# A decode step with attention and a gated MLP: chunks of T, S and PV interleaved, and w_out spread unevenly over the partitions

## Chip, core and metric

The kernel runs on one core of a Trainium2 chip. The metric is the device time of one execution in microseconds (us). Three runs of the kernel before gave 130.85, 130.9 and 132.37 us; their median, 130.9 us, is the time before.

## What is computed

One token `x` (1 x 576) is normalised, and the result goes through two branches whose outputs are added to `x`:

```
xn = layernorm(x)
A:  q = xn @ wq                       # 32 heads of 128, 16 key/value heads
    k, v = the last 4096 rows of k_cache, v_cache     # per key/value head, 4096 x 128
    o = softmax(q k^T / sqrt(128)) v ; A = o @ wo     # wo is 4096 x 576
B:  z = gelu(xn @ w_in)               # 576 x 4608
    z1, z2 = halves of z (2304 each)
    h = z1 * (w_sp * layernorm(z2) + b_sp) ; B = h @ w_out    # w_out is 2304 x 576
out = x + A + B
```

All inputs are bfloat16. With one token every matrix is used once, so the work is to read 51 MB from HBM: 16.8 MB of keys, 16.8 MB of values, 4.7 MB of wq, 5.3 MB of w_in, 4.7 MB of wo and 2.65 MB of w_out.

## The kernel before

**Loads.** SyncE (queue SP) issues every large load in the order of the list `order` (L103), and after it four loads of w_out (L117). Two key/value heads make one unit of 2 MB: `k0` to `k7` and `v0` to `v7`, each a tile of 128 partitions with 16 KB on each. `win1` to `win3` are thirds of w_in and `wo0` to `wo3` quarters of wo. All of these tiles come from the pool `units` (L60), which has 8 buffers: the ninth load can only be issued when the PE has finished with the first tile, and so on round the ring. A load reuses the semaphore of the load eight places ahead of it, so that SP also waits for that one to have landed. Behind SP's issues the loads stand in one hardware queue, spread over 16 DMA engines. Two single elements (`w_sp`, `b_sp`, L380) and the row `x` are loaded from ScalarE's queue.

**Attention by pairs of units.** Pair j is the units 2j and 2j+1. A unit has 8 chunks n of 8 blocks of 128 x 128. `T(n)` (L225) transposes the 8 blocks of a key chunk on the PE into PSUM and copies them to SBUF as kT (VectorE, or ScalarE for chunks 1, 4, 6 of eight). `S(n)` (L237) multiplies kT with the query into the scores of the pair. `sm_max`, `sm_tr`, `sm_exp` and `sm_rec` are the softmax: maximum per partition, a transpose to get it over the partitions, exponential, sum and reciprocal. `PV(b)` (L283) multiplies the 64 blocks of a value unit with the probabilities; `O_perm(j)` brings the result into the order of wo's rows, and `WO(j)` (L306) multiplies it with a quarter of wo, 32 small matmuls that accumulate in `out_ps`.

**MLP.** `z_part(b)` (L314) is a third of xn @ w_in, `gelu` runs on VectorE and ScalarE, `z_gate` (L346) makes the gated vector g and moves it from "element p + 128 c on partition p" to "18 consecutive elements on each partition" with 18 small matmuls: `row_of` (built by GpSimd, L146 to L151) holds 18 selection matrices, `col_of` (L215) the position inside a partition, and the result is `hv`. The last loop (L432) multiplies each of hv's 18 columns with the matching rows of w_out: 18 times 4 matmuls into `out_ps`. Row r of w_out's 18 on a partition sits in `wout_t[r]`, loaded in four parts of 8, 6, 3 and 1 rows.

**Order of the PE.** The order is written by hand (L396). In the part of pair j the PE first runs T of all 16 chunks of pair j+1, then S of all 16, then the stage's list: PV, z parts, permutations and WO of pair j, with the steps of the next softmax between them. After the last stage come the matmuls of w_out, one copy of `out_ps` to SBUF (L436) and the store of the output (L437).

**GpSimd** builds the identity (L121) at the very start and then `row_of`. VectorE waits for the identity before it builds the small masks (L129 to L160), and those stand in its program ahead of the normalisation of x, whose result `xe` the first projection needs (L196, L370).

Of the kernel before, what the change touches and what calls it, by code (L numbers as in the profile page):

```python
# [8 lines left out]
FP32 = mybir.dt.float32  # L9
# [21 lines left out]
OW = D // NCG  # L31
NWO = 4
FR = FH // P
UNITS = 8
KTB = 20
NEG = -1e30


# [1 line left out]
def kernel(  # L40
# [34 lines left out]
    wq_v = A_wq.rearrange("k (s c) -> (k s) c", s=2).rearrange("(p r) c -> p r c", r=NS)  # L75
    win_v = B_w_in.rearrange("k (s c) -> (k s) c", s=2).rearrange("(p r) c -> p r c", r=NS)
    wo_v = A_wo.rearrange("(j p r) n -> j p (r n)", p=P, r=8)
    wout_v = B_w_out.rearrange("(p r) n -> p r n", r=FR)


    def load_kv(store, cache, name, b, parts=1):
# [8 lines left out]
    def load_rows(store, view, name, width, cuts):  # L90
        for a, e in zip(cuts, cuts[1:]):
            t = units.tile([P, e - a, width], BF16, name=f"{name}{a}", tag="u")
            nc.sync.dma_start(t[:], view[:, a:e, :])
            for i in range(a, e):
                store[i] = t[:, i - a, :]

    def load_wo(j):
# [2 lines left out]
        wo_t[j] = t  # L100

    win_parts = {1: (0, 3), 2: (3, 6), 3: (6, 9)}
    order = ["wq1", "k0", "k1", "wq2", "k2", "k3", "v0", "win1", "v1", "win2", "k4", "k5", "v2", "win3", "v3", "wo0",  # L103
             "k6", "k7", "v4", "wo1", "v5", "wo2", "v6", "v7", "wo3"]
    for what in order:
        name, n = what.rstrip("0123456789"), what[-1]
        if name == "k":
# [6 lines left out]
            load_rows(win_t, win_v, "win", FH, win_parts[int(n)])  # L114
        else:
            load_wo(int(n))
    load_rows(wout_t, wout_v, "wout", D, (0, 8, 14, 17, 18))  # L117


    ident = const.tile([P, P], BF16, name="ident")  # L120
# [22 lines left out]
    selr = const.tile([P, 8, 8, 16], BF16, name="selr")  # L143


    row_of = const.tile([P, FR, P], BF16, name="row_of")  # L146
    nc.gpsimd.memset(row_of[:], 1.0)
    nc.gpsimd.affine_select(out=row_of[:], in_=row_of[:], compare_op=ALU.is_ge, fill=0.0, base=0,
                            pattern=[[P, FR], [-FR, P]], channel_multiplier=1)
    nc.gpsimd.affine_select(out=row_of[:], in_=row_of[:], compare_op=ALU.is_ge, fill=0.0, base=FR - 1,  # L150
                            pattern=[[-P, FR], [FR, P]], channel_multiplier=-1)  # L151
    rem = const.tile([P, 2, FR], FP32, name="rem")
    col_of = const.tile([P, FR, FR], BF16, name="col_of")
    out_ps = ps_c.tile([P, OW], FP32, name="out_ps")
    nc.vector.memset(out_ps[:], 0.0)

# [49 lines left out]
        return xe_r[:, 2 * r:2 * r + 2]  # L206

    nc.vector.tensor_copy(selr[:], ident[:].rearrange("p (q r) -> p r q", r=8).unsqueeze(2).to_broadcast([P, 8, 8, 16]))
    whole = P // FR * FR
    nc.vector.tensor_reduce(out=rem[:, 0, :], in_=ident_f[:, 0:whole].rearrange("p (q k) -> p k q", k=FR), axis=AXX, op=ALU.add)  # L210
    nc.vector.tensor_add(rem[:, 0, 0:P - whole], rem[:, 0, 0:P - whole], ident_f[:, whole:P])
    nc.vector.tensor_copy(rem[:, 1, :], rem[:, 0, :])
    rem_r = rem[:].rearrange("p a k -> p (a k)")
    for c in range(FR // 2):
        nc.vector.tensor_copy(col_of[:].rearrange("p (b c) r -> p c b r", b=2)[:, c],  # L215
                              rem_r[:, FR - 2 * c:2 * FR - 2 * c].unsqueeze(1).to_broadcast([P, 2, FR]))


    kT, s_ps, p_sb, sm = {}, {}, {}, {}
# [56 lines left out]
    def sm_rec(j):  # L276
        su = ps_m.tile([P, 8], FP32, name=f"su{j}", tag="m")
        nc.tensor.matmul(su[:], lhsT=ones_f[:], rhs=sm[j]["ss"][:].rearrange("p i c -> p (i c)"), start=True, stop=True)  # L278
        rm = work.tile([P, 8], FP32, name=f"rm{j}", tag="rm")
        nc.vector.reciprocal(rm[:], su[:])  # L280
        sm[j]["rm"] = rm

    def PV(b):  # L283
        j, i = divmod(b, 2)
        o = ps_o.tile([P, 4], FP32, name=f"o{b}", tag="o")
        for t in range(NT):
            nc.tensor.matmul(o[:], lhsT=vn[b][:, t, :], rhs=p_sb[j][:, i, t, :], start=t == 0, stop=t == NT - 1)  # L287
        with nc.allow_low_precision(reason="the attention's output is bfloat16 in the reference"):
            nc.vector.tensor_tensor(out=oTn[:, 4 * b:4 * b + 4], in0=o[:], in1=sm[j]["rm"][:, 4 * i:4 * i + 4], op=ALU.mult)  # L289

    def O_perm(j):
        op = ps_m.tile([P, 8, 8], FP32, name=f"op{j}", tag="m")
# [15 lines left out]
            out_mm(oP[:, j, r:r + 1], wo_t[j][:, D * r:D * (r + 1)])  # L308


    hv = const.tile([P, FR], BF16, name="hv")
    zacc = const.tile([P, FR, 2], FP32, name="zacc")

    def z_part(b):  # L314
# [31 lines left out]
    def z_gate(G, sz):  # L346
        sp = ps_m.tile([P, 2], FP32, name="sz_ps", tag="m")
        nc.tensor.matmul(sp[:], lhsT=ones_f[:], rhs=sz[:], start=True, stop=True)
        mz = rstd_of(sp[:], FH, "mz")
        gz = work.tile([P, FR], FP32, name="gz")  # L350
        nc.vector.tensor_scalar(out=gz[:], in0=G[:, 1, :], scalar1=mz[:, 0:1], scalar2=mz[:, 3:4],
                                op0=ALU.subtract, op1=ALU.mult)
        nc.vector.tensor_scalar(out=gz[:], in0=gz[:], scalar1=wb[:, 0:1], scalar2=wb[:, 1:2],
                                op0=ALU.mult, op1=ALU.add)
        g = work.tile([P, FR], BF16, name="g")
        nc.vector.tensor_mul(g[:], G[:, 0, :], gz[:])
        spread = const.tile([P, FR, FR], BF16, name="spread")
        nc.vector.tensor_tensor(out=spread[:], in0=col_of[:], in1=g[:].unsqueeze(2).to_broadcast([P, FR, FR]), op=ALU.mult)
        hp = ps_m.tile([P, FR], FP32, name="hp", tag="m")
        for c in range(FR):  # L360
            nc.tensor.matmul(hp[:], lhsT=row_of[:, c, :], rhs=spread[:, c, :], start=c == 0, stop=c == FR - 1)
        nc.vector.tensor_copy(hv[:], hp[:])


# [20 lines left out]
    for n in range(2 * NCH):  # L385
# [6 lines left out]

    stages = [["v0", "z1", "v1", "perm0", "z2"], ["v2", "z3", "v3", "perm1", "wo0"],  # L396
              ["v4", "wo1", "v5", "perm2", "wo2"], ["v6", "v7", "perm3", "wo3"]]
    for j, stage in enumerate(stages):
        if j == 0:
            sm_tr(0)  # L400
        if j + 1 < len(stages):
            for n in range(2 * NCH * (j + 1), 2 * NCH * (j + 2)):
                T(n)
                if n % 16 == 2 and j == 0:
                    sm_exp(0)
                if n % 16 == 8 and j == 0:
                    sm_rec(0)
            for n in range(2 * NCH * (j + 1), 2 * NCH * (j + 2)):
                S(n)
            sm_max(j + 1)  # L410
        for k, what in enumerate(stage):
            name, n = what[:-1], int(what[-1])
            if name == "v":
                PV(n)
            elif name == "z":
                z_part(n)
            elif name == "perm":
                O_perm(n)
            else:
                WO(n)  # L420
            if j + 1 < len(stages):
                if k == 0:
                    sm_tr(j + 1)
                elif k == 1:
                    sm_exp(j + 1)
                elif k == 2:
                    sm_rec(j + 1)
            if what == "z3":
                G, sz = gelu()
            if what == "v3":  # L430
                z_gate(G, sz)
    for j in range(FR):  # L432
        out_mm(hv[:, j:j + 1], wout_t[j], last=j == FR - 1)

    res = const.tile([P, OW], BF16, name="res")
    nc.vector.tensor_copy(res[0:97, :], out_ps[0:97, :])  # L436
# [31 lines left out]
```

## Time and profile before

| what | value |
|---|---|
| median of three runs | 130.9 us |
| the profiled execution, its own time | 131.38 us |
| its span, first to last instruction | 129.6 us |
| PE matmul busy | 92.8 us (72%) |
| VectorE busy | 57.8 us (45%) |
| ScalarE busy | 28.7 us (22%) |
| GpSimd busy | 7.1 us, all before 7.92 us |
| read from HBM | 50.96 MB, 393 GB/s over the span |
| mean granted TensorE clock | 0.73 |

The page of the profile gives the busy time of each engine and a picture of the span in 40 slices of 3.24 us, in tenths; the line DMA is the mean busy share of the 16 DMA engines. The chain of waits follows the work that ended last back to the start; "issue" in it is time in which the engine waited for nothing that the profile shows. A table of stretches gives for each engine the busy time and, in the last two columns, the busy share of the DMA engines and their rate in GB/s. Times in these views count from the first instruction.

### The profile page before, as it was taken

To read this page: it belongs to the slowest core of one execution; us is meant where nothing else is said; L and a number is where in the kernel's file an instruction comes from. 1 tells how busy PE (TensorE), PEld (TensorE's weight loads), DVE (VectorE), ACT (ScalarE), POOL (GpSimd) and SP (SyncE) were. 2 spreads that over 40 slices of the span, in tenths; PEclk is the share of its full clock that TensorE was granted. 3 is DMA by queue.
4 is the path that set the end of the run, shared out by engine and by line. 5 is a ranking of instruction groups with operands and counts; after the bars stand their busy time and mean duration, and the time that the engine had idled before them with its cause. 6 is when DMAs were issued, how large, how long until landed. Compare 5 with 4: busy or idle time off the path is not lost.

```text
span 129.6 us, 4571 instructions
## 1 busy us (share of the span) xinstructions
PE 92.8 (72%) x2135; PEld 86.2 (67%) x2135; DVE 57.8 (45%) x146; ACT 28.7 (22%) x34; POOL 7.1 (5%) x9
## 2 busy tenths in 40 slices
PE   3013999984798896585999993921989994878290
PEld 3013998874797786574988792921979792768190
DVE  6976758500658722252267421375367422420100
ACT  3001146500056710010155500101075400100000
POOL 7940000000000000000000000000000000000000
PEclk9999999995559996555579985555599955555555
DMA  4999999999999999999999999999999999999820
GB/s 132 430 392 438 455 415 400 445 427 420 430 416 427 431 411 425 444 410 435 420 409 438 428 411 429 430 425 425 408 431 426 416 444 415 420 402 419 333 106 0
DMA packets 4495, 51.23 MB, mean 395 GB/s; under 512 B 509, under 2 KB 638, under 8 KB 1022
## 3 DMA queue, kind: packets, MB, share of 16 engines
q1 hardware_dynamic: 4472, 50.96, 93.7%
q8 instruction: 16, 0.26, 0.8%
q14 instruction: 1, 0.01, 0.0%
q10 hardware_dynamic: 6, 0.00, 0.0%
HBM read 50.96 MB, written 0.00 MB: 393 GB/s over the span
## 4 chain that ended last, share of the span: by engine, by line
PE 57%; DVE 16%; issue 12%; ACT 11%; POOL 0%; ACTq 0%; POOLq 0%
PE tp L230 20%; PE s L245 10%; ACT kT L232 9%; PE o L287 9%; PE out_ps L303 5%; PE zp L319 3%; PE q_ps L370 3%; DVE other L141 2%; DVE d L268 2%; DVE ss L273 2%; DVE ident_f L129 2%; ACT p L270 1%; DVE own L137 1%; PE bc L264 1%; DVE kT L234 1%
## 5 line engine op out<-in xcount | busy, mean ns | idle before, releaser
L230 PE MATMUL tp<-ident,k 128*128 128x128 bf16 x512 | 39.5, 245 | 2.7 <-ACT kT L232 1.9
L230 PEld LDWEIGHTS <-k 128*128 128x128 bf16 x512 | 36.9, 113 | 5.0 <-issue 4.3
L234 DVE COPY kT<-tp 128x1024 bf16<-128x1024 bf16 x40 | 26.7, 689 | 15.1 <-PE tp L230 14.9
L232 ACT COPY kT<-tp 128x1024 bf16<-128x1024 bf16 x24 | 23.7, 1014 | 37.8 <-PE tp L230 37.7
L287 PE MATMUL o<-p,v 128*128 128x4 bf16 x512 | 15.4, 166 | 9.1 <-issue 8.8
L287 PEld LDWEIGHTS <-v 128*128 128x128 bf16 x512 | 14.5, 104 | 9.8 <-issue 9.7
L245 PEld LDWEIGHTS <-kT 128*128 128x128 bf16 x512 | 13.3, 97 | 3.1 <-issue 3.1
L245 PE MATMUL s<-q_bf,kT 128*128 128x4 bf16 x512 | 13.8, 165 | 2.1 <-issue 2.1
L270 ACT ACTIVATE p<-d 128x512 bf16<-128x512 f32 x4 | 2.5, 630 | 32.8 <-DVE d L268 32.8
L250 DVE TENSOR_REDUCE mx<-s 128x8 f32<-128x512 f32 x4 | 2.8, 692 | 14.7 <-PE s L245 14.7
L289 DVE TENSOR_TENSOR oTn<-o,rm 128x4 bf16<-128x4 f32 x8 | 1.3, 160 | 16.9 <-PE o L287 16.9
L303 PE MATMUL out_ps<-wo,oP 128*1 128x144 bf16 x128 | 4.8, 318 | 3.0 <-issue 1.8
L303 PEld LDWEIGHTS <-oP 128*1 128x1 bf16 x128 | 3.3, 113 | 3.6 <-issue 2.3
L370 PEld LDWEIGHTS <-wq 128*128 128x128 bf16 x144 | 4.1, 101 | 2.3 <-issue 2.3
L370 PE MATMUL q_ps<-xe,wq 128*128 128x2 bf16 x144 | 4.0, 164 | 2.2 <-DVE xe L196 2.2
L319 PEld LDWEIGHTS <-win 128*128 128x128 bf16 x162 | 4.9, 105 | 0.3 <-issue 0.2
L319 PE MATMUL zp<-xe,win 128*128 128x2 bf16 x162 | 4.8, 166 | 0.1
L273 DVE TENSOR_REDUCE ss<-p 128x8 f32<-128x512 bf16 x4 | 2.7, 686 | 2.8 <-ACT p L270 2.8
L168 PE MATMUL x_ps<-x,twice 64*128 64x9 bf16 x1 | 0.2, 166 | 5.3 <-DVE x L166 5.3
L168 PEld LDWEIGHTS <-twice 64*128 64x128 bf16 x1 | 0.1, 101 | 5.4 <-DVE x L166 5.4
L278 PE MATMUL su<-ss,ones_f 128*128 128x8 f32 x8 | 2.1, 332 | 1.3 <-DVE u L329 0.7
L268 DVE TENSOR_TENSOR d<-s,mb 128x512 f32<-128x512 f32 x4 | 2.8, 691 | 0.1
(94 smaller groups left out, 57.0 us busy)
## 6 DMA issues: line engine op xcount, KB each, us to landing
v<-in_A_v_cache_dram SPq DMA_DIRECT2D x8, 2048.0 KB, 24.9
k<-in_A_k_cache_dram SPq DMA_DIRECT2D x7, 2048.0 KB, 24.3
win<-in_B_w_in_dram SPq DMA_DIRECT2D x3, 1728.0 KB, 26.3
wo<-in_A_wo_dram SPq DMA_DIRECT2D x4, 1152.0 KB, 23.9
wq<-in_A_wq_dram SPq DMA_DIRECT2D x2, 2048.0 KB, 14.1
k<-in_A_k_cache_dram SPq DMA_DIRECT2D x2, 1024.0 KB, 11.1
wout<-in_B_w_out_dram SPq DMA_DIRECT2D x1, 1152.0 KB, 20.3
wout<-in_B_w_out_dram SPq DMA_DIRECT2D x1, 864.0 KB
```

The costliest lines, as they stand in the source:

```text
L230: nc.tensor.transpose(tp[:, i, :], kn[b][:, 8 * c + i, :], ident[:])
L232: nc.scalar.copy(kT[n][:], tp[:])
L234: nc.vector.tensor_copy(kT[n][:], tp[:])
L245: nc.tensor.matmul(s_ps[j][:, i, 8 * c + t, :], lhsT=kT[n][:, t, :], rhs=q_bf[:, 4 * b:4 * b + 4], start=False, stop=True, skip_group_chec ...
L250: nc.vector.tensor_reduce(out=mx[:], in_=s_ps[j][:].rearrange("p i t c -> p i c t"), axis=AXX, op=ALU.max)
L268: nc.vector.tensor_tensor(out=d[:], in0=s_ps[j][:], in1=mb[:].unsqueeze(2).to_broadcast([P, 2, NT, 4]), op=ALU.subtract)
L270: nc.scalar.activation(p[:], d[:], ACT.Exp, scale=SCALE)
L273: nc.vector.tensor_reduce(out=ss[:], in_=p[:].rearrange("p i t c -> p i c t"), axis=AXX, op=ALU.add)
L287: nc.tensor.matmul(o[:], lhsT=vn[b][:, t, :], rhs=p_sb[j][:, i, t, :], start=t == 0, stop=t == NT - 1)
L303: nc.tensor.matmul(out_ps[32 * g:32 * g + 1, :], lhsT=lhsT, rhs=rhs[:, OW * g:OW * (g + 1)], start=start, stop=last, tile_position=(0, 32 ...
L319: nc.tensor.matmul(zp[:, c, :], lhsT=win_t[r][:, P * c:P * (c + 1)], rhs=xe_of(r), start=(r == rows.start and c == 0), stop=r == rows.stop ...
L370: nc.tensor.matmul(q_ps[:, c, :], lhsT=wq_t[r][:, P * c:P * (c + 1)], rhs=xe_of(r), start=(r == 0 and c == 0), stop=r == NS - 1, skip_grou ...
```

## The change

Three things are changed together.

1. **Order of the PE.** T, S and PV of a pair are no longer three blocks. A loop over c issues T of chunk c, S of chunk c-5 and PV (now cut into chunks of 8 blocks) of chunk c-7 of the pair before. `z_gate` is split: its vector work runs at c = 1 of the last pair's loop, its 18 matmuls at c = 8. The pool of kT tiles has 16 buffers instead of 20.
2. **Order of the loads.** v1, v3 and v5 move ahead of win1, win3 and wo1.
3. **w_out.** Its first 1792 rows are spread as 14 rows on each of 128 partitions, in four loads of 7, 4, 2 and 1 rows. The next 504 rows go into a new tile `wx`: 9 rows on each of 56 partitions of the first 64, by four loads of 14 partitions each whose source has an outer dimension of 7. The last 8 rows go to partition 60 of `wx` by one load. These five loads are issued before those of w_out's first part. GpSimd clears `wx` first, ahead of the identity, and builds the selection matrices for the new layout with small instructions. The last loops take 9 columns on 64 partitions and then 14 columns on 128: 23 times 4 matmuls.

```
-KTB = 20
+KTB = 16
+RA = 14
+RB = 9
+FA = RA * P
+CB = FR - RA
...
-    wout_v = B_w_out.rearrange("(p r) n -> p r n", r=FR)
+    wout_v = B_w_out[0:FA].rearrange("(p r) n -> p r n", r=RA)
...
-    order = ["wq1", "k0", "k1", "wq2", "k2", "k3", "v0", "win1", "v1", "win2", "k4", "k5", "v2", "win3", "v3", "wo0",
-             "k6", "k7", "v4", "wo1", "v5", "wo2", "v6", "v7", "wo3"]
+    order = ["wq1", "k0", "k1", "wq2", "k2", "k3", "v0", "v1", "win1", "win2", "k4", "k5", "v2", "v3", "win3", "wo0",
+             "k6", "k7", "v4", "v5", "wo1", "wo2", "v6", "v7", "wo3"]
...
-    load_rows(wout_t, wout_v, "wout", D, (0, 8, 14, 17, 18))
+    wx = const.tile([64, RB * D], BF16, name="wx")
+    nc.gpsimd.memset(wx[:], 0.0)
+    wx_v = B_w_out[FA:FA + 56 * RB].rearrange("(a h b i r) n -> a b i h (r n)", a=2, h=2, b=2, r=RB)
+    for a in range(2):
+        for b in range(2):
+            p0 = 32 * a + b
+            nc.sync.dma_start(wx[p0:p0 + 27:2, :], wx_v[a, b])
+    nc.sync.dma_start(wx[60:61, 0:8 * D], B_w_out[FH - 8:FH].rearrange("r n -> (r n)").unsqueeze(0))
+    load_rows(wout_t, wout_v, "wout", D, (0, 7, 11, 13, 14))
...
     row_of = const.tile([P, FR, P], BF16, name="row_of")
-    nc.gpsimd.memset(row_of[:], 1.0)
-    nc.gpsimd.affine_select(out=row_of[:], in_=row_of[:], compare_op=ALU.is_ge, fill=0.0, base=0,
-                            pattern=[[P, FR], [-FR, P]], channel_multiplier=1)
...
+    nc.gpsimd.memset(row_of[:], 0.0)
+    nc.gpsimd.memset(row_of[:, 0:RA, :], 1.0)
+    nc.gpsimd.affine_select(out=row_of[:, 0:RA, :], in_=row_of[:, 0:RA, :], compare_op=ALU.is_ge, fill=0.0, base=0,
+                            pattern=[[P, RA], [-RA, P]], channel_multiplier=1)
...
+    for c in range(CB):
+        for a in range(2):
+            to = row_of[:, RA + c, 32 * a:32 * a + 28].rearrange("m (i b) -> m i b", b=4)
+            nc.gpsimd.memset(to, 1.0)
...
-    def PV(b):
+    def PV(n):
+        b, c = divmod(n, NCH)
         j, i = divmod(b, 2)
-        o = ps_o.tile([P, 4], FP32, name=f"o{b}", tag="o")
-        for t in range(NT):
-            nc.tensor.matmul(o[:], lhsT=vn[b][:, t, :], rhs=p_sb[j][:, i, t, :], start=t == 0, stop=t == NT - 1)
+        if c == 0:
+            sm[j]["o"] = ps_o.tile([P, 4], FP32, name=f"o{b}", tag="o")
+        for t in range(8 * c, 8 * c + 8):
+            nc.tensor.matmul(sm[j]["o"][:], lhsT=vn[b][:, t, :], rhs=p_sb[j][:, i, t, :], start=t == 0, stop=t == NT - 1)
...
+    def z_rows(spread, spreadB):
+        hp = ps_m.tile([P, RA + RB], FP32, name="hp", tag="m")
         for c in range(FR):
-            nc.tensor.matmul(hp[:], lhsT=row_of[:, c, :], rhs=spread[:, c, :], start=c == 0, stop=c == FR - 1)
+            lo, hi, w = (0, RA, spread[:, c, :]) if c < RA else (RA, RA + RB, spreadB[:, c - RA, :])
+            nc.tensor.matmul(hp[:, lo:hi], lhsT=row_of[:, c, :], rhs=w, start=c in (0, RA), stop=c in (RA - 1, FR - 1))
...
+    ROUND, SLAG, PLAG = 2 * NCH, 5, 7
+    parts = [["z1", "z2", "perm0"], ["z3", "perm1", "wo0"], ["wo1", "perm2", "wo2"]]
+    for j in range(1, NB // 2):
+        for c in range(ROUND + PLAG):
+            if c < ROUND:
+                T(ROUND * j + c)
+            if j == 1 and c == 0:
+                sm_tr(0)
+            if j == 1 and c == 3:
+                sm_exp(0)
+            if j == 1 and c == 5:
+                sm_rec(0)
+            if SLAG <= c < ROUND + SLAG:
+                S(ROUND * j + c - SLAG)
+            if j == 3 and c == 1:
+                spread, spreadB = z_gate(G, sz)
+            if j == 3 and c == 8:
+                z_rows(spread, spreadB)
+            if c == ROUND + SLAG - 1:
+                sm_max(j)
+            if c >= PLAG:
+                PV(ROUND * (j - 1) + c - PLAG)
+        sm_tr(j)
+        for k, what in enumerate(parts[j - 1]):
...
+    for n in range(ROUND * 3, ROUND * 4):
+        PV(n)
+    O_perm(3)
+    WO(3)
+    for r in range(RB):
+        out_mm(hv[0:64, RA + r:RA + r + 1], wx[:, D * r:D * (r + 1)])
+    for j in range(RA):
+        out_mm(hv[:, j:j + 1], wout_t[j], last=j == RA - 1)
```

## Prediction

> **What bounds the kernel now.** I read the page first: span, slices, queues.
>
> ```profile
> span 129.6 us, 4571 instructions
> ...
> DMA  4999999999999999999999999999999999999820
> GB/s 132 430 392 438 455 415 400 445 427 420 430 416 427 431 411 425 444 410 435 420 409 438 428 411 429 430 425 425 408 431 426 416 444 415 420 402 419 333 106 0
> ...
> q1 hardware_dynamic: 4472, 50.96, 93.7%
> q8 instruction: 16, 0.26, 0.8%
> ...
> q10 hardware_dynamic: 6, 0.00, 0.0%
> ```
>
> The DMA engines are full from the second slice to the 37th, at about 423 GB/s. The bytes stay the same, so no gain on an engine shortens that stretch; only the front, the tail or a hole in the queue can move the time. The queues also tell how wide a load runs. Each of the 31 loads of 128 rows leaves 16 x (8 data + 1 closing) packets, 4464; the other 8 of q1 are the store's four rows and four closings; q10's six are three loads of one row. So a load of 128 rows runs on 16 engines, one of 4 rows on 4, of one row on one.
>
> Next, a table of stretches at the end (columns: stretch, length, busy of PE, PEld, DVE, ACT, POOL, PE clock, DMA share, GB/s):
>
> ```profile
> 121.00:122.00 1.00, 0.40 (x9) 0.35 (x10) 0.00 (x0) 0.00 (x0) 0.00 (x0) 0.50 0.92 363
> 122.00:123.00 1.00, 0.35 (x8) 0.27 (x7) 0.51 (x3) 0.00 (x0) 0.00 (x0) 0.50 0.58 237
> 123.00:124.00 1.00, 0.85 (x32) 0.85 (x36) 0.09 (x1) 0.00 (x0) 0.00 (x0) 0.50 0.52 197
> 124.00:125.00 1.00, 1.00 (x44) 1.00 (x36) 0.00 (x0) 0.00 (x0) 0.00 (x0) 0.50 0.41 154
> 125.00:126.00 1.00, 1.00 (x44) 1.00 (x40) 0.00 (x0) 0.00 (x0) 0.00 (x0) 0.50 0.02 7
> ```
>
> From 122 us about half of the engines are done. The landing events of the last load say it finely: seven engines at 122.2 to 122.6 us, one at 123.4, one at 124.0, seven at 125.3 to 125.6. All carry the same bytes. Chaining the packets by their times shows why: each 16 KB packet of q8 (the PE's instructions) sets one engine back by some 1.5 us, and only eight engines take these, two each. The engine of 123.4 takes none, but is late from about 28 us on, when ScalarE's one-row loads and a small instruction load run.
>
> Third, the chain of waits at the end:
>
> ```profile
> 113.45 0.61 PE su L278 x2
> ...
> 114.82 1.13 PE out_ps L303 x32
> 115.95 1.81 PE o L287 x64
> ...
> 118.00 1.61 PE o L287 x55
> 119.61 1.96 issue
> 121.57 0.42 PE o L287 x9
> ...
> 122.22 0.37 PE op L294 x8
> ...
> 123.15 3.32 PE out_ps L303 x78
> ...
> 126.49 0.31 DVE res L436
> ```
>
> v7 has landed everywhere by 116.5 us, but the PE reaches it at 118.0 and stands 1.96 us in it: a q8 packet runs from 119.2 to 120.3, and the PE resumes 1.3 us behind its end. Such a stop comes at multiples of 128 matmul pairs (2013 here) when the PE runs short matmuls. So two things end together: the PE runs without a break to 126.46, and w_out's last load lands at 125.6 (issued at 112.9, 12.7 to landing). Both must shrink for a gain.
>
> Last, the timeline of the front, for GpSimd:
>
> ```profile
> 1.31 2.02 POOL L147 MEMSET row_of<- 128x2304 bf16 x1
> 1.40 2.01 DVE L129 CAST ident_f<-ident 128x128 f32<-128x128 bf16 x1 [0.20 <-POOL ident masks.py:199]
> ...
> 3.39 2.23 POOL L148 TENSOR_SCALAR_AFFINE_SELECT row_of<-row_of 128x2304 bf16<-128x2304 bf16 x1
> ...
> 3.83 1.84 DVE L137 COPY own<-ident 2x128 bf16<-2x128 bf16 x1
> ```
>
> VectorE starts on the identity, and its tiny copies last as long as the GpSimd instruction beside them: both end together.
>
> **The change, part by part.**
>
> *GpSimd's front.* The clearing of wx (5184 elements) goes ahead of the identity: at row_of's 2.02 us for 2304 elements, 4.5 us. The identity moves from 1.37 to 5.9 us. Behind it row_of costs 2.0 (memset) + 14/18 of 2.0 + 2 x 14/18 of 2.23 = 7.0 us instead of 6.5, and about 26 small instructions at 0.10 to 0.29 us (the constants and the identity's rows), 3 to 7 us. VectorE's three stretched copies end with GpSimd's instructions, so xe, at 12.2 us before, comes 3 to 5 us later; I take 4.5. Queued behind it: the first q part, hence T(0) and the releases of wq1 and k0. What hides it: win1 was issued at 19.63 us and landed 23 us later, so SP can be 4.5 us late without emptying the queue. It costs the end nothing if the PE regains 4.5 us by pair 3; otherwise all of it.
>
> *PE's order.* The stages run from T(16) at 33.88 to T(32) at 62.38 to T(48) at 92.28: 28.5 and 29.9 us, with PE busy 22.7 and 22.3. The holes: instruction stops of 2.56 and 2.16 in the first; 2.15 and the gelu-to-gate chain (84.9 to 90.4, PE nearly idle) in the second. The T blocks (9.5 to 11.8 us each) also wait for ScalarE's copies of 1.0 us, while S and PV (26 ns a pair) outrun the instruction loads. Mixed, S and PV fill the copy waits and the instruction loads get time. Bounds for a stage: 22.5 (the busy time) to 30 (no gain); I take 25.5. Two stages regain some 7 us, more than the 4.5. So T(48) starts when k6 has landed (86.4), and PV of v4 at c = 7 waits for v4 (96.2). From there the loads pace the PE: 16 more steps at 0.4 to 1.2 us end near 107, where PV(4) ended before (107.15); the softmax runs as before but without PV(5)'s 1.8 us, and WO(2) ends at 113 to 115 instead of 115.95. The gate's chain is hidden in the wait for v4.
>
> *Loads.* The moved v1, v3, v5 swap places of 2.8 to 4.2 us inside a queue 20 us deep: nothing. The five wx loads need no buffer but five semaphores, so w_out's first load waits for v6 (111.6) instead of going out at 101.8, the second for v7 (116.5), the third for wo3 (119.3). The slowest engine then still has 11 rows x 8 packets queued, 3.8 us, against 1.0 us from the first issue to the first packet. Zero; with the cover gone, about 1 us.
>
> *w_out's spread.* Every engine loses 4 rows on 8 partitions, 36.9 KB: at 26.4 KB a us (a 9216-byte packet takes 349 ns) 1.40 us. By the rule of widths each wx load runs on 7 engines, two rows of 10,368 bytes each: 8 packets of 0.39, 3.14 us for four loads. The 8-row load adds 0.35 us on one engine. An engine in the set so ends 1.74 us later, any other 1.40 earlier. Which seven? No row tells.
> - Best: the seven early ones: 122.6 + 1.74 = 124.35; the late ones 125.6 - 1.4 = 124.2. End 124.35.
> - Worst: some of the late ones: 125.6 + 1.74 = 127.35.
> - Between: early ones with the engine of the one-row loads, 123.43 + 1.74 + 0.35 = 125.5.
>
> I take the last: the only narrow loads whose engine can be told, ScalarE's, run on one outside the eight, and a set that starts where they do stays outside too. Then w_out ends where it ended before, 125.5 against 125.6.
>
> [...]
>
> *The last matmuls.* v6 and v7 need 3.4 us of PV; PV(7) can end at 118.4, with an instruction stop at 120. Then permutation and WO(3) as before (1.6 + 1.1 us) to 121 to 122.6. The last loops have 92 instead of 72 matmuls: 20 x 33 ns = 0.66 us; 3.0 us in all, 124 to 125.6. The loads (125.5) are then last, with four matmuls behind the last of them: the last one starts at 125.7 instead of 126.1. The rest (copy, store) is unchanged.
>
> Sum: 0 (front, regained) + 0 (loads' order) - 0.4 (tail) = span 129.2, own time 131.38 - 0.4 = 130.98. The profiled execution stands 0.48 above the median, 130.9: predicted 130.5 us.
>
> [...]
>
> **Rivals.**
> 1. *All seven are early engines.* Last landing 124.35, last matmul 124.5: -1.6, 129.3 us. For: seven end early, and seven are asked for. Against: one of the eight without instruction loads is late.
> 2. *The set holds engines that carry instructions.* 127.35, last matmul 127.5: +1.4, 132.3 us.
> 3. *Balance helps, but the PE's tail binds.* The stop at pair 2013 stays and 20 pairs come on top: +0.7, 131.6 us. There is also a new boundary, pair 2141 of now some 2155, 13 pairs before the end; its stop is up to 2 us unless the block before was entered 4.2 us earlier (121.57 to 125.8 before).
> 4. *The late start is not regained* (slower). If stages take 28 us or more, T(48) comes 4 us later and so does the end: +4, 134.9 us. It decides from T(48) later than about 90 us: the tail has 2 us of slack. Against: the holes counted above.
>
> **How the numbers follow.** Forecast 0.42, rivals 0.20, 0.18, 0.10, 0.10. Measurement tells about 2%, 2.6 us. Faster by that needs 128.3; perfect balance is worth the idle share from 122 to 125.17 us in the table, 3.17 - (0.58 + 0.52 + 0.41 + 0.02) = 1.6 us, so 0.04, from rival 1 with the PE's gain. Slower by that (133.5): most of rival 4 and a little of 2 and 3, 0.10. Within: 0.86. The forecast's own range is 130.1 to 131.0; the range 129.0 to 132.8 takes in rivals 1 to 3.
>
> **What would show it.** Right: T(48) near 86 to 90 us, a wait for v4 until 96, DMA share full to 122, w_out's last landing near 125.5 with one engine last, PE waiting for loads in the last loop. Wrong: landings ending together at 124.3 (rival 1), or seven late ones at 127 (2); an issue gap behind 120 us (3); T(48) beyond 92 (4).

## The result and the profile after

The changed kernel takes 132.88 us, the median of six runs (132.25 to 133.72), where the kernel before takes 130.97 (130.85 to 132.37): 1.0125 times as long, estimated over all the runs, with a 95% interval of 1.0091 to 1.0159 (the quotient of the two medians is 1.0146). The forecast was 130.5 us and a range from 129.0 to 132.8; the result lies just above the range. The profiled execution took 133.02 us, its span is 131.1.

The page of the profile after:

```profile
span 131.1 us, 4660 instructions
...
DMA  4999999999999999999999999999999999999600
GB/s 135 420 407 452 420 430 407 452 435 420 420 435 407 426 422 432 414 440 420 420 430 415 420 419 441 415 430 435 405 425 420 424 426 440 404 414 375 246 30 5
...
q1 hardware_dynamic: 4558, 50.96, 92.6%
q8 instruction: 17, 0.28, 0.9%
```

The bytes are the same and the engines are full just as long; the last four slices of 3.28 us hold 375, 246, 30 and 5 GB/s, where the last four of before held 419, 333, 106 and 0: the end of the stream is longer and thinner. There is one instruction packet more on q8. The table of stretches shows who trails:

```profile
122.00:123.00 1.00, 0.38 (x8) 0.32 (x9) 0.00 (x0) 0.00 (x0) 0.00 (x0) 0.50 0.76 302
...
124.00:125.00 1.00, 0.82 (x32) 0.81 (x32) 0.12 (x1) 0.00 (x0) 0.00 (x0) 0.50 0.18 71
125.00:126.00 1.00, 1.00 (x40) 0.77 (x32) 0.00 (x0) 0.00 (x0) 0.00 (x0) 0.50 0.12 48
126.00:127.00 1.00, 1.00 (x41) 0.75 (x36) 0.00 (x0) 0.00 (x0) 0.00 (x0) 0.50 0.07 25
```

Before, the share was 0.41 from 124 to 125 us and 0.02 afterwards. Now it drops to 0.18 and lasts two microseconds longer: most of the engines that ended last now end earlier, and two end later. The landing events of the last load, read engine by engine:

```
before   122.19 122.19 122.36 122.43 122.46 122.49 122.60 | 123.43 | 123.97 | 125.31 125.39 125.43 125.46 125.49 125.57 125.61
after    122.09 122.40 122.51 122.54 | 123.76 123.88 123.88 123.95 123.97 124.01 124.07 124.10 124.23 | 125.15 | 127.04 127.10
```

The chain of waits at the end:

```profile
107.95 2.00 issue
...
117.75 1.81 PE o L322 x64
119.80 1.64 PE o L322 x56
121.44 1.19 issue
...
124.18 4.12 PE out_ps L340 x89
```

The PE reaches v6's chunks at 117.75 us, later than the 115.95 of before, has its instruction stops at 107.95 and 121.44, and starts its last stretch at 124.18 instead of 123.15. That stretch is also longer, 4.12 instead of 3.32 us. So both of the things that end together, the loads and the PE, have become later: the last landing by 1.5 us (125.61 to 127.10), the last matmul by 1.8 (126.11 to 127.93). The experiments take them apart.

The front, on GpSimd:

```profile
0.79 4.41 POOL L123 MEMSET wx<- 64x5184 bf16 x1 [0.29 <-POOLq L501]
```

and on VectorE, which waits for it:

```profile
5.75 2.00 DVE L142 CAST ident_f<-ident 128x128 f32<-128x128 bf16 x1 [4.55 <-POOL ident masks.py:199]
```

Clearing takes 4.41 us, and the first projection starts at 16.89 instead of 12.16 us.

### The profile page after: what moved, and what is told of

Read it like the earlier page. It is cut to its first block, busy times and chain, and to the rows that moved or that the text cites. A ratio compares the mean times of both kernels' runs of the same rounds, so it can differ in the third digit from the quotient of the medians.

```text
span 131.1 us, 4660 instructions
## 1 busy us (share of the span) xinstructions
PE 95.2 (73%) x2155; PEld 89.1 (68%) x2155; DVE 58.8 (45%) x152; ACT 28.9 (22%) x34; POOL 18.2 (14%) x37
## 4 chain that ended last, share of the span: by engine, by line
PE 64%; DVE 16%; issue 12%; ACT 4%; POOL 0%; ACTq 0%; POOLq 0%
PE tp L263 27%; PE s L278 10%; PE o L322 9%; PE out_ps L340 6%; PE q_ps L413 3%; ACT kT L265 2%; PE zp L356 2%; PE su L311 2%; DVE mx L283 2%; DVE d L301 2%; DVE ss L306 2%; DVE other L154 2%; DVE ident_f L142 2%; DVE kT L267 1%; ACT p L303 1%
## 5 line engine op out<-in xcount | busy, mean ns | idle before, releaser
L263 PE MATMUL tp<-ident,k 128*128 128x128 bf16 x512 | 46.2, 256 | 2.3 <-DVE kT L267 1.2
L263 PEld LDWEIGHTS <-k 128*128 128x128 bf16 x512 | 39.0, 117 | 3.4 <-issue 3.2
L267 DVE COPY kT<-tp 128x1024 bf16<-128x1024 bf16 x40 | 27.3, 690 | 22.7 <-PE tp L263 22.5
L265 ACT COPY kT<-tp 128x1024 bf16<-128x1024 bf16 x24 | 24.1, 1012 | 45.2 <-PE tp L263 45.2
L278 PE MATMUL s<-q_bf,kT 128*128 128x4 bf16 x512 | 20.9, 166 | 3.4 <-issue 3.4
L322 PE MATMUL o<-p,v 128*128 128x4 bf16 x512 | 19.9, 165 | 3.0 <-issue 2.8
L278 PEld LDWEIGHTS <-kT 128*128 128x128 bf16 x512 | 18.8, 101 | 4.7 <-issue 4.7
L322 PEld LDWEIGHTS <-v 128*128 128x128 bf16 x512 | 16.7, 100 | 3.6 <-issue 3.5
L311 PEld LDWEIGHTS su<-ss,ones_f 128*128 128x128 f32 x8 | 1.9, 304 | 4.9 <-DVE ss L306 4.9
L123 POOL MEMSET wx<- 64x5184 bf16 x1 | 4.4, 4412 | 0.3 <-POOLq L501 0.3
L142 DVE CAST ident_f<-ident 128x128 f32<-128x128 bf16 x1 | 2.0, 2005 | 4.5 <-POOL ident masks.py:199 4.5
```

Of the source, the lines that this page charges most:

```text
L123: nc.gpsimd.memset(wx[:], 0.0)
L142: nc.vector.tensor_copy(ident_f[:], ident[:])
L263: nc.tensor.transpose(tp[:, i, :], kn[b][:, 8 * c + i, :], ident[:])
L265: nc.scalar.copy(kT[n][:], tp[:])
L267: nc.vector.tensor_copy(kT[n][:], tp[:])
L278: nc.tensor.matmul(s_ps[j][:, i, 8 * c + t, :], lhsT=kT[n][:, t, :], rhs=q_bf[:, 4 * b:4 * b + 4], start=False, stop=True, skip_group_chec ...
```

## The experiments

All times are medians; the ratios are estimated over all runs, against the kernel before on the same chip. Where the intervals of two rows overlap, the difference between them is not clear of the spread. One table first, so that each run can be placed. "First q" is the start of the first projection on the PE, T(48) the first transpose of the last pair, "last landing" the last engine's landing of w_out's last load, "last matmul" its start; all are of the profiled execution.

| kernel | first q | T(48) | last landing | last matmul | median | ratio (95%) |
|---|---|---|---|---|---|---|
| before | 12.16 | 92.21 | 125.61 | 126.11 | 130.97 | 1 |
| changed | 16.89 | 90.82 | 127.10 | 127.93 | 132.88 | 1.0125 (1.0091 to 1.0159) |
| reorder only | 12.15 | 87.34 | 125.85 | 125.90 | 131.12 | 0.9991 (0.9972 to 1.0011) |
| spread only | 16.87 | 95.68 | 127.27 | 128.53 | 134.68 | 1.0259 (1.0209 to 1.0309) |
| late clearing | 12.54 | 86.48 | 127.35 | 127.40 | 132.40 | 1.0081 (1.0049 to 1.0113) |
| last pair in blocks | 16.88 | 90.01 | 127.31 | 127.40 | 132.54 | 1.0108 (1.0059 to 1.0158) |
| 64 partitions, every second | 15.86 | 90.33 | 125.63 | 127.12 | 132.40 | 1.0109 (1.0043 to 1.0176) |
| 16 rows, five engines | 16.96 | 90.23 | 125.22 | 127.92 | 133.70 | 1.0210 (1.0166 to 1.0254) |
| 17 rows, five engines | 13.99 | 87.51 | 125.27 | 125.90 | 130.91 | 0.9984 (0.9959 to 1.0010) |

My theory after the result: the narrow loads' set holds two engines that carry instruction packets (the second rival). Against it stands the fourth: the late start, which the PE does not regain.

**Reorder only.** The changed kernel with w_out, `row_of` and `col_of` as before:

```
-    wx = const.tile([64, RB * D], BF16, name="wx")
...
-    load_rows(wout_t, wout_v, "wout", D, (0, 7, 11, 13, 14))
+    load_rows(wout_t, wout_v, "wout", D, (0, 8, 14, 17, 18))
```

> The interleaved order of PE and loads with w_out spread as before (18 rows on 128 partitions, no wx, no clearing of it). Theory PE tail (the interleaved last pair ends its scores 5 us later and leaves its softmax uncovered, and the 20 extra matmuls come on top): WO(3) starts near 124.2 us as in the changed kernel, then 104 instead of 124 matmuls, so the copy of out_ps near 127.6 instead of 128.3; about 0.7 us under the changed kernel, 1.1 us above the kernel before. Theory loads (the narrow loads' late end sets the time): w_out's last landing is back at 125.6 and the time at the kernel before's, 0 difference. Theory front (the late clearing of wx sets all): also back at the kernel before's.

131.12 us against 131.13. Its chain of waits ends:

```profile
109.82 15.66 DMA wout<-in_B_w_out_dram
...
125.53 0.68 PE out_ps L313 x16
```

The chain runs through the load, not through the PE: T(48) comes 4.9 us earlier than before, and nothing of that reaches the end, because the last landing (125.85) is where it was. The interleaved order makes room on the PE and the loads take it.

**Spread only.** The order of before with the new layout and clearing.

```
-    load_rows(wout_t, wout_v, "wout", D, (0, 8, 14, 17, 18))
+    wx = const.tile([64, RB * D], BF16, name="wx")
+    nc.gpsimd.memset(wx[:], 0.0)
...
+    load_rows(wout_t, wout_v, "wout", D, (0, 7, 11, 13, 14))
```

> The kernel before with only the new spread of w_out (wx, its clearing ahead of the identity, the five narrow loads, 92 last matmuls; 16 kT buffers). Theory PE tail: WO(3) starts where it did before or a little later, 20 more matmuls: +0.7 us. Theory loads: the last landing is 127.3 us instead of 125.6: +1.4 us. Theory front: the 4.4 us of the clearing are not regained in the block order: +4 us.

134.68 us. Here the fourth rival is true: T(48) comes 3.5 us later than before, and the PE's last matmul starts at 128.5, behind a last landing of 127.27. The block order regains little of the 4.7 us.

**Late clearing.** The changed kernel with `wx` cleared behind `row_of`, and its loads behind that in the program, in the same place of SP's order.

```
-    wx = const.tile([64, RB * D], BF16, name="wx")
-    nc.gpsimd.memset(wx[:], 0.0)
...
+    wx = const.tile([64, RB * D], BF16, name="wx")
+    nc.gpsimd.memset(wx[:], 0.0)
     remA = const.tile([P, 2, RA], FP32, name="remA")
```

> The changed kernel with the clearing of wx placed behind the building of row_of on GpSimd, so that the identity is ready at 1.4 us again; the order of the loads is the same. Theory front: T(0) is back at 14 us and the time 1 to 2 us lower. Theories PE tail and loads: T(0) back at 14 us, but the last pair's loop is held by its own chain and by v4, so at most 0.5 us lower.

132.40 us, some 0.5 less than the change; the two intervals overlap (up to 1.0113 here, from 1.0091 there), so that this gain is not clear of the spread. The front is back (12.54), T(48) is the earliest in the table, and still the end is late. Its chain:

```profile
119.38 7.62 DMA wout<-in_B_w_out_dram
...
127.04 0.67 PE out_ps L340 x11
```

The PE stands waiting for the load: the loads alone, with the front repaired, cost 132.40 - 131.12 = 1.28 us against the reordered kernel.

**The first interleaved stage.** No run was made for it, but the traces show what it consists of. The stretch from T(16) to T(32) in the kernel before, in the changed one and with late clearing (the last three columns are the granted clock, the DMA share and GB/s):

```profile
33.67:62.24 28.57, 22.80 (x511) 21.48 (x510) 12.51 (x28) 7.23 (x8) 0.00 (x0) 0.68 1.01 425
36.40:66.54 30.14, 26.01 (x512) 24.84 (x512) 12.91 (x29) 7.22 (x8) 0.00 (x0) 0.56 1.01 425
32.86:61.67 28.81, 21.31 (x512) 20.18 (x512) 12.78 (x29) 7.22 (x8) 0.00 (x0) 0.80 1.01 426
```

The same work keeps the PE busy for 22.8, 26.0 and 21.3 us, at mean granted clocks of 0.68, 0.56 and 0.80. In the changed kernel the loop runs without a hole from 46.55 to 56.79 us at a clock of 0.50, and a step of T, S and PV takes 1.28 us; in the reordered kernel, at 1.00 (46.23 to 50.47), it takes 0.85. Where the clock is high, with late clearing, holes open instead: the PE stands for 2.12 us inside the loop (from 49.47) and for 2.50 behind it (from 55.55), and the stage takes 28.8 us all the same. What sets the granted clock, no run here tells.

**Last pair in blocks.** The changed kernel, with T, S and PV of the last pair in blocks again.

```
-    for j in range(1, NB // 2):
+    for j in range(1, NB // 2 - 1):
...
+    for c in range(ROUND):
+        T(ROUND * 3 + c)
...
+    for c in range(ROUND):
+        S(ROUND * 3 + c)
```

> The changed kernel, but the last pair's T, S and PV in blocks as before (T of 16, S of 16, maximum, PV(4), WO(1), exponential, PV(5) in the softmax's wait); pairs 1 and 2 stay interleaved; gate at the second T, its matmuls at the ninth. Theory PE tail: WO(2) ends near 115 instead of 117.75 and the PE's end would come 2 us earlier, but the loads' last landing at 127.4 then holds it: 0.4 to 0.6 us under the changed kernel. Theory loads: the same 0.4 or nothing. Theory front: no difference.

132.54 us, the interval overlapping the change's. The last matmul comes at 127.40 instead of 127.93, and there it stands 0.1 us behind the last landing (127.31). So with these loads the order of the last pair can cost the end 0.5 us at most; the load holds it there.

**A short PV.** The kernel before, with 448 of the 512 matmuls of PV left out, so its attention sums only every eighth block.

```
-        for t in range(NT):
+        for t in range(0, NT, 8):
```

> The kernel before with only every eighth block in PV (448 of 512 matmuls left out, all loads as they were). If the PE's instruction packets set engines back, there are 12 or 13 of them instead of 16, and the landings of w_out's last load show four engines (not seven) two steps late, about four one step late at 124 us, and the rest early at 122.3 us. If the spread of the landings has another cause, seven are late again.

One run: 130.97 us, beside 130.98 for before. The chain holds the load:

```profile
104.35 20.94 DMA wout<-in_B_w_out_dram
```

The PE had 448 pairs less to do and the end did not move: before, too, the loads bind. With 13 instead of 16 packets on q8 the landings changed as the packets would have it: eight engines to 123.33 us as before, four at 123.89 to 124.17, and only four instead of seven at 125.38 to 125.67. So a q8 packet does set its engine back by some 1.5 us.

**Rows of equal width.** Can the balance be had without choosing engines? The last 512 rows as 8 rows on each of the first 64 partitions, by one load:

```
+    wx = const.tile([MB, RB * D], BF16, name="wx")
+    nc.sync.dma_start(wx[:], B_w_out[FA:FH].rearrange("(m r) n -> m (r n)", r=RB))
```

> The changed kernel with the last 512 rows of w_out as 8 rows on each of 64 partitions, by one load of 64 partitions (one outer dimension of 64) in place of the five narrow ones; no clearing of wx is needed then, so the identity is early again. 88 last matmuls. Theory loads: all 16 engines share it, w_out's last landing goes from 127.4 back to 125.7 and the time to that of the reorder alone, 131.1 us. Theory PE tail: the loads' end does not matter; 16 more matmuls than the reorder alone, 0.5 us above it.

A miss: 135.57 us (1.0354; 1.0318 to 1.0391), last landing near 130. The table of stretches (DMA share and GB/s in the last two columns):

```profile
116.00:118.00 2.00, 1.75 (x66) 1.69 (x64) 0.16 (x1) 0.00 (x0) 0.00 (x0) 0.50 1.00 230
118.00:120.00 2.00, 1.60 (x56) 1.51 (x55) 0.00 (x0) 0.00 (x0) 0.00 (x0) 0.50 1.03 207
```

The engines are busy all the time and move half of what they moved before; packets of 9216 bytes, 349 ns elsewhere, take 0.68 us here (the middle one of those from 116 to 122 us; 0.43 to 1.17). Either rows on 64 partitions are slow, or these 64 are.

**Every second partition** asks that: the same load onto partitions 0, 2, 4 and so on to 126, the tile cleared late. If the first 64 are slow, the rate should stay near 420 GB/s here and the time come to 131 to 132 us; if rows on 64 partitions are, the rate should fall to some 220 GB/s again and the time be 135 to 136.

```
-    nc.sync.dma_start(wx[:], B_w_out[FA:FH].rearrange("(m r) n -> m (r n)", r=RB))
+    nc.sync.dma_start(wx[0:P - 1:2, :], B_w_out[FA:FH].rearrange("(m r) n -> m (r n)", r=RB))
```

> The kernel with the last 512 rows as 8 rows on 64 partitions, but on every second of the 128 partitions instead of on the first 64; the tile is cleared by GpSimd behind the selection matrices, and the eight added columns are multiplied over all 128 partitions (zeros between). [...]

```profile
116.00:118.00 2.00, 2.00 (x71) 1.75 (x64) 0.21 (x1) 0.00 (x0) 0.00 (x0) 0.50 1.03 432
118.00:120.00 2.00, 1.75 (x66) 1.69 (x64) 0.16 (x1) 0.00 (x0) 0.00 (x0) 0.50 0.99 409
```

The rate is whole and the last landing is 125.63: it was the first 64 partitions. With the load on these, 207 to 236 GB/s were measured from 116 to 124 us, 223 in the mean; what makes them slower, no run here shows. The wide load behind is held up as well: its packets of 8064 bytes take 0.45 to 0.67 us on average there, and 0.31 with every second partition. The time missed its expectation, 132.40 instead of 131 to 132, and the timeline of this kernel's front shows a likely reason:

```profile
11.83 3.93 POOL L165 MEMSET wx<- 128x4608 bf16 x1
...
11.82 3.99 DVE L214 TENSOR_SCALAR xe<-x9f,mv,rpar 128x5 bf16<-128x5 f32 x4
```

The clearing, moved back, now runs beside the making of xe, which takes 3.99 us with it and 0.87 where the clearing comes later (late clearing: from 15.85 us on, xe from 11.78). The first q came at 15.86 us, and the PE's last matmul at 127.1, 1.5 us behind the loads.

**Four engines**, and the same with ScalarE's one-element loads issued at the start:

```
+    wx_v = B_w_out[FA:FH].rearrange("(h i r) n -> i h (r n)", i=NARROW, r=RB)
+    nc.sync.dma_start(wx[:], wx_v)
```

> 16 rows of w_out on every partition and 8 on 32 partitions by one load whose source has an outer dimension of 4 (32 packets of 9216 bytes); no clearing of wx. By 26.4 KB a us every engine loses 0.70 us of w_out and the four of the narrow load get 2.8. If these four carry no instruction packets, the last landing is 124.9 to 125.5 and the time 0.1 to 0.7 us under the reorder alone (131.1). If one or two of them carry instruction packets, it is 125.6 + 2.1 = 127.7 and the time 2 us above it.

> The same as the run with four engines, with ScalarE's two one-element loads issued right behind x's row at the start. If the lag of one engine from 28 us on comes from these two loads, its closing packet in the last load moves to the group of the early ones (0.8 us earlier), and the time falls by 0.3 to 0.7 us if that engine was last; if the lag is the small instruction load's, no difference.

133.29 us (1.0149 to 1.0200) and 133.60 (1.0174 to 1.0227). Both told little of their question: the narrow load fills the first 32 partitions here, the rate falls to between 222 and 331 GB/s from 116 to 122 us, and the last landings are 127.8 and 128.2. Why it falls with four engines was not taken apart. But the second settles something: its small loads ran at 5.4 to 7.2 us, and the engine that trails by 1.1 us was still there, from about 39 us on, behind an 8 KB instruction packet of another queue (q14) at 37.6.

**Which engines?** The reordered kernel with seven tiny loads of 1 to 7 rows, first into one tile, then into seven:

```
+        if what == "v6":
+            for m in range(1, 8):
+                probe = const.tile([64, D], BF16, name=f"probe{m}")
+                nc.sync.dma_start(probe[0:4 * m - 3:4, :], B_w_out[8 * m:8 * m + m])
```

> The reordered kernel with the old layout of w_out, plus seven tiny loads of 1, 2, ... 7 rows of 1152 bytes (8 KB apart in their own partitions) between the loads of v6 and v7; nothing reads them. Each is to run on as many engines as it has rows. Theory A (a load of m rows takes the same first m engines each time, and two of the first seven carry instruction packets): the landings of the seven loads nest; the load of 7 rows has four landings early, one about 1.1 us behind them and two about 3 us behind, as the narrow loads of the changed kernel had (116.8 to 117.0, 118.2, 120.1 us); the first load whose landings show a late one tells the place of the first carrying engine in the order. Theory B (a load starts on whatever engine is next): the classes of the landings change from load to load without nesting, and the change's mix of four, one and two was chance. The time itself: within 0.5 us of the reordered kernel's, 131.1.

> As the kernel with the seven tiny loads of 1 to 7 rows, but each into a tile of its own: into one shared tile each had waited for the one before it, 2 us apiece, and met idle engines, so their landings told nothing but that the load of one row came with the early engines (108.15 us, where v6 landed on the early engines at 107.97 to 108.6 and on the one-row loads' engine at 109.3). Theory A (a load of m rows takes the same first m engines; two of the first seven carry instruction packets): the landings nest, the load of 7 rows shows four early ones, one about 1.1 us behind and two about 3 us behind, and the load of one row an early one. Theory B (a load starts on whatever engine is next): no nesting. Time: within 1 us of the reordered kernel's 131.1, since the seven loads now stand in the queue together.

The first try took 142.18 us and told nothing: in one tile the loads waited for each other, 2 us apiece, and the queue ran dry. The second took 135.24 (its expectation of 131 to 132 was a miss; SP came to its next load only at 111.7 us, and the queue ran dry here too), but its landings answer:

```
rows  landing of each engine (v6, ahead in the queue: 108.1 to 108.3 early, 109.36 one, 109.8 to 111.7 the others)
1     108.46
2     108.24 108.64
3     108.37 108.42 108.82
4     108.54 108.60 109.00 109.54
5     108.33 108.72 108.76 109.17 109.72
6     108.52 108.89 108.94 109.35 109.90 111.61
7     108.70 109.06 109.11 109.53 110.08 111.81 111.82
```

They nest: each row adds one engine to those of the row above, and those move on by 0.2 us. In this order the engines are early, early, early, the one that trails by 1.1 us, early, and then two carriers. So a load of seven rows has two carriers (engines that carry the PE's instruction packets) in it, as each of the four seven-engine loads of the changed kernel had, and one of five has none. No trace here numbers the engines.

**Five of the engines, first try.** 16 (or 17) rows on all partitions, the last 256 (128) rows as 8 (4) on 32 partitions, by loads with outer dimensions of 5 and of 3.

```
+    for p0, u0, k in ((0, 0, 5), (32, 20, 3)):
+        rows = B_w_out[FA + u0 * RB:FA + (u0 + 4 * k) * RB]
+        nc.sync.dma_start(wx[p0:p0 + 4 * k, :], rows.rearrange("(i s r) n -> i s (r n)", i=k, s=4))
```

> The change with another spread: 16 rows on all 128 partitions, and the last 256 rows as 8 rows on 32 partitions by two loads whose source has an outer dimension of 5 and of 3; each of the five engines writes its own partitions, and GpSimd clears the narrow tile behind the selection matrices. The first five engines carry no instruction packets in the nested loads. Every engine loses two rows on 8 partitions, 0.70 us; the first three get 64 rows of 1152 bytes, 2.80 us, the fourth (the one-row loads' engine) and the fifth 32 rows, 1.40 us. Theory A (the set decides): carriers end at 125.5 - 0.70 = 124.8 us, the first three at 122.4 + 2.10 = 124.5, the fourth at 123.5 + 0.70 = 124.2; last landing 124.6 to 125.1; the PE then binds with its 96 last matmuls, behind 122.7 us at the earliest: 125.9 to 127, and the time is 130.5 to 131.5, against 132.4 for the change with a late clearing. Theory B (narrow loads as such hold the stream up): a landing behind 126 us and 132.0 to 132.8.

> As the kernel before, with 17 rows on all partitions and 128 rows as 4 rows on the 32 partitions: carriers end at 125.5 - 0.35 = 125.15 us, the first three at 122.4 - 0.35 + 1.40 = 123.45, the fourth at 123.8; 84 last matmuls, 12 fewer, 0.4 us. Theory A: last landing 124.9 to 125.4, time 130.3 to 131.0, the best of all these kernels or level with the kernel before. Theory B: a landing behind 126 us and 131.5 or more.

135.81 us (1.0274 to 1.0366) and 132.03 (1.0038 to 1.0078). By numbers alone theory B had won. But the loads landed on ten and twelve engines: i and s lie one behind the other in the source and merge into one dimension of 20 or 12 rows. These sets held carriers, and with 16 rows the rate fell to 226 and 198 GB/s in two of the stretches. It tested something else than it was meant to.

**Second try,** with the source turned so that the dimensions cannot merge:

```
-        nc.sync.dma_start(wx[p0:p0 + 4 * k, :], rows.rearrange("(i s r) n -> i s (r n)", i=k, s=4))
+        nc.sync.dma_start(wx[p0:p0 + 4 * k, :], rows.rearrange("(s i r) n -> i s (r n)", i=k, s=4))
```

> The kernel with 16 rows on all and 8 rows on 32 partitions, with one change: the source's row order is turned so that its two dimensions cannot be merged. In the kernel before they merged into 20 and 12 rows, and the two loads ran on 10 and 12 engines (their landings), carriers among them, into partitions of other engines. Now the outer dimensions of 5 and 3 stand, and each engine writes its own partitions. Theory A (set and paths decide): the two loads land on five and three engines; last landing 124.6 to 125.3 us, no stretch under 360 GB/s before 122 us, time 130.5 to 131.7, bounded by the PE's 96 last matmuls. Theory B (narrow loads as such hold the stream up): stretches of 200 to 300 GB/s again, a landing behind 126 us, time 132 or more.

> The same turn in the kernel with 17 rows on all and 4 rows on 32 partitions. Theory A: the two loads land on five and three engines; last landing 124.9 to 125.4 us (carriers 0.35 us earlier than in the reordered kernel's 125.4 to 125.85), time 130.3 to 131.0. Theory B: a landing behind 126 us and 131.5 to 132.3.

Now the loads land on five and three engines, and the last landings are 125.22 and 125.27, inside both expectations. (The rate before 122 us is 354 GB/s at the least with 16 rows, where 360 was expected, and 381 with 17.) No engine is past 125.3, with the same kind of narrow loads: the set makes the loss on the loads' side. Which partitions an engine writes, no trace shows, so what lowered the rate in the first try stays open. The totals differ. With 17 rows it is 130.91 us, level with the kernel before (0.9959 to 1.0010), 1.97 below the change. Its chain:

```profile
121.65 3.63 PE out_ps L332 x81
125.28 0.56 issue
125.84 0.30 PE out_ps L332 x5
```

With 16 rows it is 133.70, a miss of 2 us, though its loads end as early:

```profile
124.13 4.05 PE out_ps L330 x90
...
128.21 0.31 DVE res L475
```

Its PE ends at 128.2 on its own: first q at 16.96 instead of 13.99 us, T(48) 2.7 us later, the last stretch begun 2.5 us later, and 12 matmuls more. Its clearing runs from 12.22 to 16.15 us, and VectorE turns to xe at 16.12; with 17 rows it takes 2.01 us and is over at 13.2. So the PE starts as late as in the change (16.89) and its last matmul comes as late (127.92 and 127.93), with other loads: this is the late start, unhidden.

## Why the prediction failed, step by step

- **The bound of before: right.** The loads and the PE end together; the reordered kernel and the short PV, where a PE with less to do changes nothing, show that the loads are the last of the two.
- **The size of the late start: right.** 4.7 us measured, 4.5 predicted, clearing 4.41 for 4.5.
- **"Two stages regain some 7 us": wrong, the first step that failed.** T(48) came at 90.82 us, not 86.4. The first interleaved stage took 30.1 us (36.40 to 66.54) where 25.5 was taken, no less than a block stage, and the second 24.3; the reordered kernel has 30.2 and 24.9. Of the 4.7 us by which the front stands behind that kernel's, 4.1 are left at T(32), 3.5 at T(48), 1.8 at the end of S and 1.6 at the end of PV: what is regained is regained late. WO(2) ended at 117.75, not at 113 to 115. The mis-sized term is the first stage. Its lower bound, the busy time of 22.5 us, was read at the granted clock of before; at 0.56 the PE alone was busy for 26.0, and at 0.80 (late clearing) holes of 2.1 and 2.5 us were left that the mix was to fill.
- **The loads' order at nothing: right**, since the reordered kernel contains it. The later issue of w_out's loads behaved as priced: the early engines outside the set ended at 122.1 to 122.5 instead of 122.4 - 1.4 = 121.0, a wait of 1.1 to 1.5 us, on engines that are not last. (win1's last engine landed 24.8 us behind its issue, where the prediction read 23; nothing hangs on it.)
- **"I take the last": wrong, the second step that failed.** The terms of the spread were right: to 0.1 us for the trailing engine, 125.15 (123.43 + 1.74), and for the carriers inside the set, 127.04 and 127.10 (125.4 + 1.74), and to 0.4 for the nine landings from 123.76 to 124.23, in which carriers outside the set (125.5 - 1.4) and early ones inside it (122.4 + 1.74) lie together. The set was wrong. It was chosen by the engine that trails by 1.1 us, taken for that of ScalarE's one-row loads. In the changed kernel these ran at 31.7 to 33.0 us, and no engine trailed by 1.1 in the load that landed at 38.3 to 40.4; the first to show it landed at 43.2 to 45.2, behind the packet of q14 at 40.7. In the kernel with 17 rows and the turned source q14's packet comes first, at 20.4, and the load that landed at 22.4 to 24.1 already shows the engine, at 23.68, before the one-row loads run (28.9 to 30.7). In the kernel before both fall close together (26.0 and 27.5 to 28.7 us), which is why they looked like one cause. The load of one row in the nested series came with the early engines. So the worst case of the three, 127.35, was the true one for the loads: 127.1, though with two late engines, where the prediction's sign for it was seven.
- **The last matmuls: right in size.** The last stretch grew from 3.32 to 4.12 us, 0.80 for 0.66. The stop at the new boundary did not come in the change; in the kernel with 17 rows a hole of 0.56 us stands there. Before, the stop of 1.96 us cost the end some 0.4 us at most: w_out's last engine landed at 125.61 there, and in the short PV, where the PE waits for that load, the last matmul starts at 125.73 instead of 126.11.
- **The total.** Two costs lie side by side in the changed kernel: w_out's last landing at 127.10, and the PE, late from the front, whose last matmul comes at 127.93. The second rival said 132.3 with a landing at 127.35; the late clearing is that case (127.35, 132.40, the PE waiting), while in the change itself the PE ends behind the loads. Taking away the late front alone brought 0.5 us, not clear of the spread; taking away the carriers alone (16 rows, 133.70) brought nothing; both together (17 rows, where the start is 1.8 us late and 8 matmuls fewer stand at the end) brought 2.0. The forecast gave the fourth rival all or nothing; it came in part, with T(48) at 90.82, just past the 90 us from which it was to decide.

## What to carry to other kernels

Where a stream of loads ends the kernel, look at each engine's last landing and not at the mean share: an uneven load can bring the end forward only if it goes to engines that end early (last landing 125.22 us on five without instruction packets, 127.10 on seven with two carriers among them), and a nested series of tiny loads into separate tiles shows which those are. Even the right set bought no time here (130.91 us, level with before): the last landing moved by 0.3 to 0.6 us. When two ends lie within a microsecond, price a change on both, since each hides the other's cost and taking away one looks like nothing. A busy time holds for the clock at which it was read (one stage: 22.8, 26.0 and 21.3 us at 0.68, 0.56 and 0.80); as a bound for another order it needs that clock beside it. Count the landings of a narrow load, since dimensions that merge change the engines (ten and twelve instead of five and three here), and look at the rate while it runs: the same 512 rows moved at 207 to 236 GB/s or at 409 to 432, by the partitions alone.

## What the runs showed of the hardware

- By the landings, eight of the 16 DMA engines carried the PE's instruction packets, in turn, at some 1.5 us per packet. The kernel before has 15 of them in the full stream and a 16th at 123.4 us: seven engines land two steps late, one a single step (123.97). The short PV has 12 and a 13th at 123.8: four land two steps late, four one.
- In a load of 64 rows, 16 engines that write into the first 64 partitions move 207 to 236 GB/s at a busy share of 1; into every second of the 128 partitions 409 to 432.
- A load whose dimensions stay apart with an outer one of 7, 5 or 3 ran on 7, 5 or 3 engines (the changed kernel, and the second try of five engines); merged rows of 20 and 12 ran on 10 and 12 (the first try).
- The PE stops at the same places of its program, multiples of 128 pairs (a matmul and its weight load) apart, to within one: 351, 735, 863, 1246, 1758 and 2014 in the kernel before. At pair 2014 or 2015 the hole is 1.2 to 2.8 us in most of these kernels, 4.6 in the one with rows on the first 64 partitions and 0.1 in spread only.
- A step of T, S and PV of a chunk took 1.28 us at a granted clock of 0.50 (the changed kernel, 46.55 to 56.79 us) and 0.85 at 1.00 (reorder only, 46.23 to 50.47).
